# DeltaNet and SwiGLU on one core: the first inverse Z transposed as blocks side by side, spread by four masks, a quarter of it on GpSimd

## The chip, the cores and the metric

One core of a Trainium2 chip runs the kernel. The metric is the device time of one execution in microseconds (us). Three runs of the kernel before took 661.51, 661.8 and 662.65 us; their median is 661.8 us.

## The reference

Inputs: q, k, v of shape (4, 8, 768, 48) (batch, heads, positions, width), beta of (4, 8, 768), and three weights. All is float32.

```
k_n = k / (norm(k) + 1e-6)
for t in range(S):                       # S = 768, state (B, H, 48, 48) from zero
    y[t]  = q[t] @ state
    state = state + beta[t] * outer(k_n[t], v[t] - k_n[t] @ state)
x = y as (B*S, H*D) = (3072, 384)
out = (silu(x @ w_gate) * (x @ w_val)) @ w_out     # d_ff = 1536
```

## The kernel before, in words

The recurrence is computed in 12 chunks of 64 positions. Within a chunk, the sequential update is a triangular system: the matrix of products of the keys, scaled by beta over the squared norms, is inverted once, and then the chunk is matrix products. There are 32 pairs of batch and head, so a chunk has 32 matrices of 64x64. Two batches share the 128 partitions, 64 rows each. Once a chunk's output is there, the feed-forward part of its 256 tokens (gate, value, output) fills TensorE, while the next chunk's recurrence is woven in between.

The order of the instructions on each engine is written by hand (a manual schedule): each engine takes its instructions in the order of the program text, and waits at semaphores for the other engines. SyncE (SP) issues most of the transfers, in program order too.

The start is special, because nothing can fill TensorE until chunk 0 is through. The steps of it that matter here, in program order:

- `first_tiles` clears tiles and makes row masks from the identity (`m_rows`, and `m_low`, their negatives).
- `turned(c, ...)` transposes K or Q of a chunk on TensorE (L484) and ScalarE copies the result out of PSUM (L486, L488). `first_gram` multiplies K by itself; `first_diag` takes the 32x32 diagonal blocks into one tile, `flat`, by masks. `gram` and `gram_steps` do the products of later chunks and of Q with K (L498), with ScalarE copies (L518, L523).
- `low_copies(c, ...)` writes what lies below the 16x16 diagonal blocks of chunk c into `l_sb[c]`, negated by `m_low`: six ScalarE instructions (L667) for each of chunks 0 and 1, which share this first inversion.
- VectorE transposes `flat` in 32x32 blocks into `mb` (L1950). Afterwards a partition holds one matrix, and its elements lie along the free axis.
- `first_scale` multiplies by beta over the squared norms (L675, L680) and GpSimd writes the diagonal into `zb` (L676). `first_substitution` then inverts the 16x16 blocks by forward substitution: 15 steps of two VectorE instructions each (L700, L706).
- `first_z` transposes back (L710), and `spread_z` writes the blocks into `ztp[0]`, the operand Z of the products, with a mask that keeps the blocks on the diagonal (L723 on ScalarE, L725 on VectorE); chunk 0's part is spread here, chunk 1's inside `first_advance`.
- `unread(n, p)` issues n products (L633) whose result nobody reads. They keep TensorE occupied.
- `n_products` multiplies `l_sb` by Z (L733). It opens `first_advance`, the chain of products and copies by which chunk 0 becomes the input of the feed-forward part (L952, L1040); the first feed-forward products are L1562.

Beside this, `stage(n, after)` brings in weight pieces. For a piece with `after`, GpSimd copies one word (L261) of an earlier piece's place into the new place, so that the piece's transfer (L262, on SP) is issued only once the earlier piece has landed:

```
if after is not None:
    nc.gpsimd.tensor_copy(place[:, 0:1], staged[after][:, 0:1])
queue.dma_start(out=place, in_=...)
```

The loop that stages pieces 0 to 5 stands behind `first_scale` and ahead of `first_substitution`; `power_step` (L274, L280, ScalarE) and `convert` (L293, L301, L313, VectorE) later turn a landed piece into the weights used. GpSimd also masks the Q products of chunk 0 (`under_mask`, L537).

Of the kernel before, what the change touches and what calls it, by code (L numbers as in the profile page):

```python
# [8 lines left out]
FP32 = mybir.dt.float32  # L9
U32 = mybir.dt.uint32  # L10
ALU = mybir.AluOpType
ACTF = mybir.ActivationFunctionType

C = 64
DP = 64
R = 32
# [4 lines left out]
def kernel(  # L21
# [25 lines left out]
    nc = tc.nc  # L47
# [4 lines left out]
    NB = B // 2  # L52
# [5 lines left out]
    HH = NB * H  # L58
# [3 lines left out]
    const = ctx.enter_context(tc.tile_pool(name="const", bufs=1))  # L62
# [60 lines left out]
    ztp = [const.tile([128, 2, HH, C], FP32, name=f"zt{i}") for i in range(ZB)]  # L123
# [55 lines left out]
    def load_v(c):  # L179
        vin[c] = work.tile([128, 2, NB, NJ, D], FP32, name="vin", bufs=2)  # L180
        for b in range(2):
            src = halves(v, c, b).rearrange("bp (j par) p d -> par p (bp j) d", par=2)
            for par in range(2):
                s = half_of(b ^ par if c > 1 else b).start
                nc.sync.dma_start(  # L185
                    out=vin[c][s : s + 64, par].rearrange("p bp j d -> p (bp j) d"),
                    in_=src[par],
                )
# [28 lines left out]
    staged, powers, places = {}, {}, {}  # L217

    def words(tile_):
# [3 lines left out]
    places = {  # L223
        "z0": zt_flat[0],
        "z1": zt_flat[1],
        "wo": words(wo_sb).rearrange("p t d -> p (t d)"),
    }
    H_ = PIECE
# [12 lines left out]
    for n, (name, lo) in enumerate(place_of):  # L241
        m = 2 * pieces[n][4]
# [7 lines left out]
        at = max(before) if before else LATE.get(name, -1)  # L250
# [78 lines left out]
    for b in range(2):  # L329
        rows = mask_q[64 * b : 64 * b + 64]  # L330
        nc.gpsimd.affine_select(
            out=rows,
# [5 lines left out]
            channel_multiplier=-1,  # L338
        )

    m_rows = const.tile([128, 4], FP32, name="m_rows")
    m_low = const.tile([128, 3], FP32, name="m_low")
    m_two = const.tile([128, 4, 2], FP32, name="m_two")

    p_places = [const.tile([128, 1024], FP32, name=f"p_sb{i}") for i in range(2)]
    spent, late_loads = [], []
# [105 lines left out]
    def banks(name, tag):  # L452

        if type(tag) is int:
            return [ps_ffn([128, 512], name, tag + i) for i in range(2)]
        p = ps_pair(name, tag)
        return [p[:, 0], p[:, 1]]
# [86 lines left out]
    def gram(*args):  # L544
        for _ in gram_steps(*args):
            pass
# [11 lines left out]
    def new_mb():  # L558
        return work.tile([128, R, R], FP32, name="mb", bufs=1)
# [41 lines left out]
    def pairs_of_blocks(flat):  # L601

        v = flat.rearrange("p (b n) -> p b n", b=2)[:, :, 0 : B16 * R]
        return v.rearrange("p b (k i) -> p b k i", i=R)

    def first_tiles():
        a = work.tile([128, C * 2 * HH], FP32, name="a_sb")
        for c in range(2):
            l_sb[c] = a[:, R * R * c : R * R * (c + 1)].rearrange(
                "p (h k) -> p h k", k=C  # L610
            )
        first_of["flat"] = new_mb().rearrange("p k i -> p (k i)")
        first_of["zb"] = places["z1"].bitcast(FP32)[:, 4 * H_ - 1056 : 4 * H_]
        first_of["mb"] = places["wo"].bitcast(FP32)[:, 2 * H_ : 2 * H_ + 1056]
        nc.vector.memset(first_of["zb"], 0.0)
        for c in range(2):
            nc.vector.memset(l_sb[c][:, :, 48:C], 0.0)
        for x, rows in enumerate((slice(16, C), slice(R, C), slice(48, C), slice(0, R))):
            nc.vector.tensor_reduce(
                out=m_two[:, x],  # L620
                in_=ident.rearrange("p (b n) -> p b n", b=2)[:, :, rows],
                axis=mybir.AxisListType.X,
                op=ALU.add,
            )
        nc.vector.tensor_tensor(
            out=m_rows, in0=m_two[:, :, 0], in1=m_two[:, :, 1], op=ALU.add
        )
        nc.vector.tensor_scalar_mul(m_low, m_rows[:, 0:3], -1.0)

    def unread(count, p, m=512):  # L630

        for _ in range(count):
            nc.tensor.matmul(p[0:R, 0:m], half, half[:, 0:1].to_broadcast([128, m]))  # L633
# [11 lines left out]
    def first_diag(c, p, between=None):  # L645
        to = first_of["flat"].rearrange("p (j c par h) -> p c par j h", c=2, par=2, j=R)
        to = to[:, c]
        p = [p_h.rearrange("p x h j -> p x j h") for p_h in p]
        for par in range(2):
            nc.scalar.mul(to[:, par], p[par][:, 0], m_rows[:, 3:4])  # L650
            if between and par == 0:
                between()
        for par in range(2):
            nc.vector.scalar_tensor_tensor(
                out=to[:, par],
                in0=p[par][:, 1],
                scalar=m_rows[:, 1:2],
                in1=to[:, par],
                op0=ALU.mult,
                op1=ALU.add,  # L660
            )

    def low_copies(c, p):
        l_v = l_sb[c].rearrange("p (par h) k -> p par h k", par=2)
        for par in range(2):
            for x in range(3):
                nc.scalar.mul(  # L667
                    l_v[:, par, :, B16 * x : B16 * x + B16],
                    p[par][:, x // 2, :, B16 * (x % 2) : B16 * (x % 2) + B16],
                    m_low[:, x : x + 1],  # L670
                )

    def first_scale(r_b):
        zb, b = first_of["zb"], beta_b[:, 0]
        nc.vector.tensor_tensor(out=b, in0=b, in1=r_b, op=ALU.mult)  # L675
        nc.gpsimd.tensor_copy(zb[:, 0 : R * R : R + 1], b)  # L676
        mb = pairs_of_blocks(first_of["mb"])[:, :, :, 0:B16]
        for x in range(2):
            at = slice(B16 * x, B16 * x + B16)
            nc.vector.scalar_tensor_tensor(  # L680
                out=mb[:, x],
                in0=mb[:, x],
                scalar=-1.0,
                in1=b[:, None, at].to_broadcast([128, B16, B16]),
                op0=ALU.mult,
                op1=ALU.mult,
            )

    def first_substitution():

        zb, mb = pairs_of_blocks(first_of["zb"]), pairs_of_blocks(first_of["mb"])
        for j in range(B16 - 1):
            m = B16 - 1 - j
            shape = [128, 2, m, j + 1]
            t_v = tmp_of[nc.vector][:, 0 : 2 * (j + 1) * m].rearrange(
                "p (b i k) -> p b i k", b=2, i=m
            )
            z_v = zb[:, :, j + 1 : B16, 0 : j + 1]
            m_v = mb[:, :, j : j + 1, j + 1 : B16].rearrange("p b o i -> p b i o")
            nc.vector.tensor_tensor(  # L700
                out=t_v,
                in0=zb[:, :, j : j + 1, 0 : j + 1].to_broadcast(shape),
                in1=m_v.to_broadcast(shape),
                op=ALU.mult,
            )
            nc.vector.tensor_tensor(out=z_v, in0=z_v, in1=t_v, op=ALU.add)  # L706

    def first_z():
        z = new_mb().rearrange("p k i -> p (k i)")
        nc.vector.transpose(z, first_of["zb"][:, 0 : R * R])  # L710
        first_of["z"] = z.rearrange("p (i m) -> p i m", i=R)

    def spread_z(c, x, engine, bps=slice(0, NB)):

        def by_bp(t):
            t = t.rearrange("p (par bp j) i -> p par bp j i", par=2, bp=NB)[:, :, bps]
            return t.rearrange("p par bp j i -> p par (bp j) i")

        z_v = by_bp(first_of["z"].rearrange("p i (c h) -> p c h i", c=2)[:, c])
        out = by_bp(ztp[0][:, c, :, R * x : R * x + R])  # L720
        mask = m_rows[:, 1:2] if x else m_rows[:, 3:4]
        if engine is nc.scalar:
            nc.scalar.mul(out, z_v, mask)  # L723
        else:
            engine.tensor_scalar_mul(out, z_v, mask)  # L725

# [213 lines left out]
    def first_advance():  # L940
# [63 lines left out]
        for bp in range(NB):  # L1004
# [6 lines left out]
            )  # L1011
            plus(uu[:, :, bp], t[:, 1:3, bp], pairs[bp])
        spread_z(1, 0, nc.vector)
        held_loads[26] = lambda: load_v(2)
        yield
        pq = p_sb.pop(0)
# [25 lines left out]
            if bp == 0:  # L1042
                unread(1, banks("p_t", 0)[1], 256)
        unread(1, banks("p_t", 0)[1], 256)
        spread_z(1, 1, nc.scalar)
        yield
        p_s = of_state(0, uu)
        nc.scalar.copy(state, p_s)
# [870 lines left out]
    with tc.manual_schedule(  # L1919
# [26 lines left out]
        spread_beta(copy_a)  # L1946
        turned(0, True, 0)
        low_copies(0, p_g[0])
        low_copies(1, p_g[1])
        nc.vector.transpose(first_of["mb"][:, 0 : R * R], first_of["flat"])  # L1950
        r_b = first_n()
        first_scale(r_b)
# [4 lines left out]
        turned(2, False, "py")  # L1957
        first_q = [gram_steps(0, True, 0, (copy_a, copy_a))]
        next(first_q[0])
        gram(2, False, "px", (copy_a, copy_a))  # L1960
        turned(3, False, "py")
        turned(1, True, "px")
# [1 line left out]
        first_q.append(gram_steps(1, True, "px", (copy_a, copy_a)))  # L1964
        next(first_q[1])
        next(first_q[0])
        unread(4, banks("p_t", 2)[0])
        first_substitution()
        first_z()
        some, others = slice(0, 1), slice(1, NB)  # L1970
        spread_z(0, 1, nc.scalar, some)
        spread_z(0, 0, nc.vector, some)
        spread_z(0, 0, nc.vector, others)
        spread_z(0, 1, nc.vector, others)
        scale_v(0)
        next(first_q[1])
        next(first_q[0])
# [129 lines left out]
```

## Time and profile before

| | |
|---|---|
| median of 3 runs | 661.8 us (661.51 to 662.65) |
| profiled execution, its own time | 663.32 us |
| its span, first to last instruction | 661.6 us |
| mean granted TensorE clock | 0.995 |
| TensorE busy | 649.8 us |
| VectorE, ScalarE, GpSimd busy | 475.0, 281.3, 198.7 us |

The times of single instructions come from the one profiled execution. PE is TensorE, PEld its weight loads, DVE is VectorE, ACT ScalarE, POOL GpSimd, SP SyncE (SPq: its queue of transfers). A number such as L733 is a line of the kernel; in the changed kernel the same code stands a few lines earlier or later. In a timeline a row gives the start, the length, the engine, the line, what is written and read, and in brackets the idle time ahead of it and what ended it. The granted clock is 1.00 at full TensorE speed.

### The profile page before, as it was taken

To read this page: it belongs to the slowest core of one execution; us is meant where nothing else is said; L and a number is where in the kernel's file an instruction comes from. 1 tells how busy PE (TensorE), PEld (TensorE's weight loads), DVE (VectorE), ACT (ScalarE), POOL (GpSimd) and SP (SyncE) were. 2 spreads that over 40 slices of the span, in tenths; PEclk is the share of its full clock that TensorE was granted. 3 is DMA by queue.
4 is the path that set the end of the run, shared out by engine and by line. 5 is a ranking of instruction groups with operands and counts; after the bars stand their busy time and mean duration, and the time that the engine had idled before them with its cause. 6 is when DMAs were issued, how large, how long until landed. Compare 5 with 4: busy or idle time off the path is not lost.

```text
span 661.6 us, 24916 instructions
## 1 busy us (share of the span) xinstructions
PE 649.8 (98%) x10854; PEld 596.5 (90%) x10854; DVE 475.0 (72%) x989; ACT 281.3 (43%) x626; POOL 198.7 (30%) x312
## 2 busy tenths in 40 slices
PE   8989999999999999999999999999999999999997
PEld 4667888767999999999999999999999999999997
DVE  6779699999689767758667758667758655655563
ACT  4887757224435433434532533532433432333230
POOL 8030041013894032880031881030882000000000
PEclk8989999999999999999999999999999999999999
DMA  9659763005742451364464264364263442232220
GB/s 138 144 165 265 214 145 119 1 14 92 201 78 73 97 122 51 84 142 89 99 127 92 61 152 104 81 131 105 62 142 88 93 109 67 58 97 65 81 72 25
DMA packets 147438, 68.57 MB, mean 104 GB/s; under 512 B 123456, under 2 KB 126560, under 8 KB 147328
## 3 DMA queue, kind: packets, MB, share of 16 engines
q1 hardware_dynamic: 144832, 66.28, 42.8%
q8 instruction: 85, 1.39, 0.9%
q10 hardware_dynamic: 2240, 0.59, 0.5%
q0 software_dynamic: 256, 0.10, 0.2%
q14 instruction: 25, 0.20, 0.1%
HBM read 59.08 MB, written 7.86 MB: 101 GB/s over the span
## 4 chain that ended last, share of the span: by engine, by line
PE 86%; DVE 7%; SPq 3%; issue 2%; DMA 1%; ACT 1%; POOL 0%; DVEq 0%; ACTq 0%; POOLq 0%
PE ffn L1405 39%; PE ffn L1682 21%; PE ffn L1562 9%; PE ffn L1591 2%; SPq L139 2%; PE p_px L1167 2%; PE p_py L498 1%; DVE x_t L583 1%; DVE zb L589 1%; PE p_px L921 1%; PE p_py L1069 1%; PE p_py L1086 1%; PE p_px L1150 1%; PE p_px L498 1%; SPq L185 1%
## 5 line engine op out<-in xcount | busy, mean ns | idle before, releaser
L1405 PE MATMUL ffn<-x_t,w_gv 128*128 128x128 f32 x800 | 108.7, 279 | 0.9 <-DVE p_sb L1632 0.8
L1405 PEld LDWEIGHTS ffn<-x_t,w_gv 128*128 128x128 f32 x800 | 97.4, 192 | 4.1 <-DVE p_sb L1632 2.0
L1439 ACT ACTIVATE sil<-ffn 128x256 f32<-128x256 f32 x100 | 36.4, 383 | 115.3 <-PE ffn L1405 108.0
L1405 PE MATMUL ffn<-x_ffn,w_gv 128*128 128x128 f32 x640 | 84.6, 275 | 0.0
L1682 PE MATMUL ffn<-wo_sb,h_f 128*128 128x192 f32 x480 | 83.9, 328 | 0.0
L1682 PEld LDWEIGHTS ffn<-wo_sb,h_f 128*128 128x128 f32 x480 | 77.9, 190 | 0.6
L1405 PEld LDWEIGHTS ffn<-x_ffn,w_gv 128*128 128x128 f32 x640 | 78.0, 192 | 0.3
L820 POOL TENSOR_TENSOR n_b<-mb,half 128x32 f32<-128x32 f32 x5 | 27.9, 5582 | 161.4 <-DVE mb L552 161.4
L583 POOL TENSOR_TENSOR h_f<-zb,mb 128x31 f32<-128x31 f32 (+15 forms) x124 | 69.4, 559 | 19.2 <-PE p_py L798 6.0
L589 POOL TENSOR_TENSOR zb<-zb,h_f 128x31 f32<-128x31 f32 (+15 forms) x124 | 70.8, 571 | 9.7
L1405 PE MATMUL ffn<-x_t,h_f 128*128 128x128 f32 x472 | 64.7, 280 | 0.0
L1405 PEld LDWEIGHTS ffn<-x_t,h_f 128*128 128x128 f32 x472 | 57.3, 192 | 1.6 <-DVE ffn L1632 0.5
L1440 DVE TENSOR_TENSOR h_f<-sil,ffn 128x256 f32<-128x256 f32 x100 | 39.3, 418 | 24.0 <-ACT sil L1439 24.0
L1101 ACT COPY x_ffn<-p_py 32x256 f32<-32x256 f32 (+3 forms) x108 | 39.4, 365 | 29.0 <-PE p_py L1086 27.3
L1632 DVE TENSOR_TENSOR ffn<-p_sb,ffn 128x512 f32<-128x512 f32 x40 | 27.8, 696 | 25.9 <-PE ffn L1405 25.2
L1635 DVE TENSOR_TENSOR ffn<-ffn,p_sb 128x512 f32<-128x512 f32 x40 | 27.5, 691 | 19.9 <-PE ffn L1405 19.0
L1682 PE MATMUL ffn<-last_k,h_f 128*128 128x192 f32 x200 | 36.0, 327 | 0.0
L1635 DVE TENSOR_TENSOR o_sb<-o_sb,ffn 128x192 f32<-128x192 f32 x50 | 17.5, 350 | 24.2 <-PE ffn L1682 23.5
L1562 PE MATMUL ffn<-x_t,w_gv 128*128 128x256 f32 x144 | 33.9, 385 | 0.2 <-DVE x_t L1041 0.2
L1682 PEld LDWEIGHTS ffn<-last_k,h_f 128*128 128x128 f32 x200 | 32.9, 190 | 0.1
L1562 PE MATMUL ffn<-x_ffn,w_gv 128*128 128x256 f32 x144 | 31.9, 380 | 0.0
L1405 PE MATMUL ffn<-x_ffn,h_f 128*128 128x128 f32 x232 | 30.9, 276 | 0.0
(330 smaller groups left out, 1171.8 us busy)
## 6 DMA issues: line engine op xcount, KB each, us to landing
h_f<-w_s SPq DMA_DIRECT2D x81, 256.0 KB, 2.8
more_w<-w_s SPq DMA_DIRECT2D x27, 256.0 KB, 2.7
vin<-in_v_dram SPq DMA_DIRECT2D x48, 96.0 KB, 3.5
out_dram<-o_sb SPq DMA_DIRECT2D x46, 96.0 KB, 2.2
kn<-in_k_dram SPq DMA_DIRECT2D x20, 192.0 KB, 4.5
zt<-in_moe_w_out_dram SPq DMA_DIRECT2D x10, 384.0 KB, 4.2
qpad<-in_q_dram SPq DMA_DIRECT2D x36, 64.0 KB, 3.0
w_s<-h_f SPq DMA_DIRECT2D x7, 256.0 KB, 2.6
```

What stands on the lines that cost most here:

```text
L139: dmas[b % len(dmas)].dma_start(out=t[64 * b : 64 * b + 64, :, :, 0:D].rearrange("p bp h d -> p (bp h) d"), in_=halves(x, c, b).rearrange( ...
L583: engine.tensor_tensor(out=t_v, in0=zb[:, 0 : j + 1, j : j + 1].to_broadcast([128, j + 1, m]), in1=mb[:, j : j + 1, j + 1 : R].to_broadcas ...
L589: engine.tensor_tensor(out=zb[:, 0 : j + 1, j + 1 : R], in0=zb[:, 0 : j + 1, j + 1 : R], in1=t_v, op=ALU.add,)
L820: nc.gpsimd.tensor_tensor(out=n, in0=mb.rearrange("p j i -> p (j i)")[:, 0 : R * R : R + 1], in1=half, op=ALU.pow,)
L1101: nc.scalar.copy(x_all[at % 128 : at % 128 + rows, at // 128].rearrange("p (bp b i) -> p bp b i", bp=NB, b=2), p[64 * half + lo : 64 * hal ...
L1405: nc.tensor.matmul(p[:, u], w(u), moving, start=start and u == 0, stop=True, skip_group_check=True,)
L1439: nc.scalar.activation(silu_of, p[:, 0:2], ACTF.Silu)
L1440: nc.vector.tensor_tensor(out=h_of(c, PAIRS[r][e % 3], e // 3), in0=silu_of, in1=p[:, 2:4], op=ALU.mult)
L1562: nc.tensor.matmul(ps[name][:, i], w_sb[:, t, (f + i) * 128 : (f + i + 1) * 128], xts[c][:, t], start=(t == 0 and i == 0), stop=(t == KT - 1),
L1632: nc.vector.tensor_tensor(out=out, in0=a, in1=b, op=ALU.subtract)
L1635: nc.vector.tensor_tensor(out=out, in0=a, in1=b, op=ALU.add)
L1682: nc.tensor.matmul(p[x, part], a(f - f % 2)[:, f % 2], b(f), start=not begun and f == 0, stop=f == FH - 1, skip_group_check=True,)
```

## The change

- The 16x16 blocks of `zb` are laid out side by side (16 rows of 32 columns) instead of on the diagonal of 32x32; the transpose takes 512 columns instead of 1024, and the clearing 528 instead of 1056.
- The result is spread by four masks, one for each 16 rows of 64 (three new masks in `m_rows`), into 16 columns each, instead of two masks into 32 columns each. For chunk 0 ScalarE does one quarter, GpSimd one, VectorE two; for chunk 1 VectorE and ScalarE do two each.
- The negative sign of the scaled blocks moves into the masks of `first_diag`; `first_scale` scales only the columns that the substitution reads, rows 0 to 3 on VectorE and rows 4 to 14 on GpSimd, and the diagonal is copied by VectorE.
- `low_copies(1, ...)` is split into two parts of three ScalarE instructions and moved behind the Q product of chunk 0 and behind the copies of that product. The four `unread` products after it go to the bank pair `py` instead of bank 2.

```diff
@@ first_tiles
-        first_of["zb"] = places["z1"].bitcast(FP32)[:, 4 * H_ - 1056 : 4 * H_]
+        first_of["zb"] = places["z1"].bitcast(FP32)[:, 4 * H_ - 528 : 4 * H_]
...
-        for x, rows in enumerate((slice(16, C), slice(R, C), slice(48, C), slice(0, R))):
+        starts = (slice(16, C), slice(R, C), slice(48, C), slice(0, R))
+        quarters = [slice(B16 * x, B16 * x + B16) for x in range(3)]
+        for x, rows in enumerate(list(starts) + quarters):
...
-        nc.vector.tensor_scalar_mul(m_low, m_rows[:, 0:3], -1.0)
+        nc.vector.tensor_scalar_mul(m_low, m_rows[:, 0:4], -1.0)
@@ first_diag
-            nc.scalar.mul(to[:, par], p[par][:, 0], m_rows[:, 3:4])
+            nc.scalar.mul(to[:, par], p[par][:, 0], m_low[:, 3:4])
...
-                scalar=m_rows[:, 1:2],
+                scalar=m_low[:, 1:2],
...
-    def low_copies(c, p):
+    def low_copies(c, p, pars=range(2)):
@@ first_scale
-        nc.gpsimd.tensor_copy(zb[:, 0 : R * R : R + 1], b)
-        mb = pairs_of_blocks(first_of["mb"])[:, :, :, 0:B16]
-        for x in range(2):
-            at = slice(B16 * x, B16 * x + B16)
-            nc.vector.scalar_tensor_tensor(
-                out=mb[:, x],
-                in0=mb[:, x],
-                scalar=-1.0,
-                in1=b[:, None, at].to_broadcast([128, B16, B16]),
-                op0=ALU.mult,
-                op1=ALU.mult,
-            )
+        diag = zb[:, 0 : B16 * (R + 1)].rearrange("p (i n) -> p n i", i=B16)
+        b_v = b.rearrange("p (x i) -> p x i", x=2)
+        nc.vector.tensor_copy(diag[:, 0 : B16 + 1 : B16], b_v)
+        mb = pairs_of_blocks(first_of["mb"])
+        for engine, js in ((nc.vector, slice(0, 4)), (nc.gpsimd, slice(4, B16 - 1))):
+            m = mb[:, :, js, js.start + 1 : B16]
+            in1 = b_v[:, :, None, js.start + 1 : B16].to_broadcast(list(m.shape))
+            engine.tensor_tensor(out=m, in0=m, in1=in1, op=ALU.mult)
@@ first_substitution
-        zb, mb = pairs_of_blocks(first_of["zb"]), pairs_of_blocks(first_of["mb"])
+        zb = first_of["zb"][:, 0 : B16 * R].rearrange("p (i x k) -> p x i k", x=2, k=B16)
+        mb = pairs_of_blocks(first_of["mb"])
@@ first_z
-        z = new_mb().rearrange("p k i -> p (k i)")
-        nc.vector.transpose(z, first_of["zb"][:, 0 : R * R])
+        z = new_mb().rearrange("p k i -> p (k i)")[:, 0 : B16 * R]
+        nc.vector.transpose(z, first_of["zb"][:, 0 : B16 * R])
@@ spread_z
-        mask = m_rows[:, 1:2] if x else m_rows[:, 3:4]
+        z_v = first_of["z"][:, c]
+        out = ztp[0][:, c, :, B16 * y : B16 * y + B16]
+        mask = m_rows[:, 4 + y : 5 + y] if y < 3 else m_rows[:, 2:3]
...
+        elif engine is nc.gpsimd:
+            mask = mask[:, :, None].to_broadcast([128, HH, B16])
+            engine.tensor_tensor(out=out, in0=z_v, in1=mask, op=ALU.mult)
@@ first_advance
         spread_z(1, 0, nc.vector)
+        spread_z(1, 1, nc.vector)
...
-        spread_z(1, 1, nc.scalar)
+        spread_z(1, 2, nc.scalar)
+        spread_z(1, 3, nc.scalar)
@@ the order at the start
         low_copies(0, p_g[0])
-        low_copies(1, p_g[1])
...
         next(first_q[0])
+        low_copies(1, p_g[1], (0,))
         gram(2, False, "px", (copy_a, copy_a))
...
         next(first_q[0])
-        unread(4, banks("p_t", 2)[0])
+        low_copies(1, p_g[1], (1,))
+        unread(4, banks("p_t", "py")[0])
         first_substitution()
         first_z()
-        some, others = slice(0, 1), slice(1, NB)
-        spread_z(0, 1, nc.scalar, some)
-        spread_z(0, 0, nc.vector, some)
-        spread_z(0, 0, nc.vector, others)
-        spread_z(0, 1, nc.vector, others)
+        spread_z(0, 3, nc.scalar)
+        spread_z(0, 2, nc.gpsimd)
+        spread_z(0, 0, nc.vector)
+        spread_z(0, 1, nc.vector)
```

More of the change, by code (lines that the diff above doesn't have):

```diff
@@ L339 @@
         )
-    m_rows = const.tile([128, 4], FP32, name="m_rows")
-    m_low = const.tile([128, 3], FP32, name="m_low")
-    m_two = const.tile([128, 4, 2], FP32, name="m_two")
+    m_rows = const.tile([128, 7], FP32, name="m_rows")
+    m_low = const.tile([128, 4], FP32, name="m_low")
+    m_two = const.tile([128, 7, 2], FP32, name="m_two")
     p_places = [const.tile([128, 1024], FP32, name=f"p_sb{i}") for i in range(2)]
@@ L661, in first_diag @@
             )
-    def low_copies(c, p):
+    def low_copies(c, p, pars=range(2)):
         l_v = l_sb[c].rearrange("p (par h) k -> p par h k", par=2)
-        for par in range(2):
+        for par in pars:
             for x in range(3):
@@ L708, in first_z, with spread_z @@
     def first_z():
-        z = new_mb().rearrange("p k i -> p (k i)")
[L710 to L720, printed above, removed]
-        mask = m_rows[:, 1:2] if x else m_rows[:, 3:4]
+        z = new_mb().rearrange("p k i -> p (k i)")[:, 0 : B16 * R]
+        nc.vector.transpose(z, first_of["zb"][:, 0 : B16 * R])
+        first_of["z"] = z.rearrange("p (i c h) -> p c h i", i=B16, c=2)
+    def spread_z(c, y, engine):
+        z_v = first_of["z"][:, c]
+        out = ztp[0][:, c, :, B16 * y : B16 * y + B16]
+        mask = m_rows[:, 4 + y : 5 + y] if y < 3 else m_rows[:, 2:3]
         if engine is nc.scalar:
             nc.scalar.mul(out, z_v, mask)
+        elif engine is nc.gpsimd:
+            mask = mask[:, :, None].to_broadcast([128, HH, B16])
+            engine.tensor_tensor(out=out, in0=z_v, in1=mask, op=ALU.mult)
         else:
```

## The prediction

> **What bounds the kernel now.** I read the page first (share of each engine), then busy time by stretches of the span, then the timeline around the changed lines engine by engine, then the order and the semaphore waits of the changed program's instructions. On the page:
>
> ```profile
> PE 649.8 (98%) x10854; PEld 596.5 (90%) x10854; DVE 475.0 (72%) x989; ACT 281.3 (43%) x626; POOL 198.7 (30%) x312
> ```
>
> TensorE is busy nearly throughout, so what counts is when it starts its dense work and where it stands still. The stretches (us; busy time and instructions of PE, PEld, DVE, ACT, POOL; granted clock; DMA share; GB/s):
>
> ```profile
> 25.00:30.00 5.00, 5.00 (x111) 2.17 (x104) 3.15 (x5) 3.50 (x8) 0.67 (x3) 1.00 0.45 133
> 30.00:35.00 5.00, 3.73 (x198) 3.18 (x189) 3.77 (x8) 4.28 (x11) 2.90 (x4) 1.00 0.43 136
> 35.00:41.70 6.70, 5.69 (x130) 3.75 (x129) 4.24 (x11) 5.18 (x13) 0.91 (x6) 0.75 0.41 123
> 41.70:50.00 8.30, 7.63 (x209) 6.16 (x210) 6.62 (x18) 8.24 (x22) 2.22 (x6) 1.00 0.68 207
> 50.00:60.00 10.00, 10.00 (x282) 8.38 (x281) 9.86 (x33) 7.96 (x22) 0.34 (x1) 1.00 0.99 236
> ```
>
> All that the change touches lies before 48 us. From 41.7 us TensorE has only some 3 us of idle time until 600 us, none of it put down to a transfer, so a shift of the dense work is a shift of the end. Between 28.8 and 41.7 us runs the chain of chunk 0 (products, copies, products) that leads there. It starts with `n_products` (L733). What holds it? The timeline of TensorE alone:
>
> ```profile
> 24.15 1.16 PE L498 MATMUL p_px<-qt,kt 64*64 64x64 f32 x64
> 25.24 3.63 PE L633 MATMUL ffn<-half 128*32 128x512 f32 x8
> 28.80 1.16 PE L733 MATMUL ffn<-zt,a_sb 64*64 64x64 f32 x64
> 29.78 0.63 PE L952 MATMUL p_px<-vin,zt 64*64 64x48 f32 x32
> ```
>
> L733 follows the four filler products (L633, `unread`) without a gap. Its operand Z was ready earlier, as the timeline of VectorE and ScalarE shows:
>
> ```profile
> 24.90 1.25 DVE L710 STREAM_TRANSPOSE mb<-zt 128x1024 f32<-128x1024 f32 x1
> 26.18 0.75 ACT L723 ACTIVATE zt<-mb,m_rows 128x256 f32<-128x256 f32 x1
> 26.18 1.15 DVE L725 TENSOR_SCALAR zt<-mb,m_rows 128x256 f32<-128x256 f32 x3
> ```
>
> Z is done at 27.33 us, 1.47 us ahead of L733: a faster Z alone brings nothing. Now GpSimd, which gets a quarter of Z:
>
> ```profile
> 15.40 0.50 POOL L676 COPY zt<-beta_b 128x32 f32<-128x32 f32 x1 [1.00 <-DVE beta_b L675]
> 25.96 0.19 POOL L261 COPY h_f<-h_f 128x1 uint32<-128x1 uint32 x1 [10.06 <-DMA h_f<-in_moe_w_gate_dram]
> 27.95 0.29 POOL L261 COPY h_f<-h_f 128x1 uint32<-128x1 uint32 x1 [1.80 <-DMA h_f<-in_moe_w_val_dram]
> 28.89 0.18 POOL L261 COPY h_f<-h_f 128x1 uint32<-128x1 uint32 x1 [0.65 <-DMA h_f<-in_moe_w_gate_dram]
> 32.10 0.18 POOL L261 COPY h_f<-h_f 128x1 uint32<-128x1 uint32 x1 [3.02 <-DMA h_f<-in_moe_w_val_dram]
> 32.24 2.77 POOL L537 TENSOR_TENSOR p_sb<-p_sb,mask_q 128x512 f32<-128x512 f32 x2
> ```
>
> The four L261 copies are the one-word copies of `stage(2)` to `stage(5)`, each waiting until a weight piece has landed (pieces 0, 1, 2, 3). They stand ahead of `first_substitution` in the program. In the changed program's order the new spread on GpSimd is the instruction right behind the fourth of them, and the first `n_products` matmul has a wait on GpSimd that it did not have.
>
> **The change part by part.**
>
> Masks and clearing: three more reductions (L619, 0.53 us for four, so +0.4 us) and a half-size memset of `zb` (0.94 us for 1056 columns). VectorE then idles 1.94 us for K at 5.71 us: nothing.
>
> `first_scale`: out go two scalings on VectorE (0.77 us) and GpSimd's copy of the diagonal (0.50 us, to 15.90 us). In come, on VectorE, a copy of 32 columns (about 0.2, as L675 0.19) and a product of 120 columns (L700 of 128x120, 0.28), and on GpSimd a product of 242 columns beside them (L583 of up to 247 columns averages 0.80, so about 0.7). The substitution, which began at 16.24, begins near 15.9; GpSimd's rows are first read in its fifth step, which came 2.1 us after its first. Gain about 0.35 us, or a loss of 0.3 if VectorE and GpSimd hold each other up; either way it is spent in front of a wait with slack.
>
> Transpose: 512 columns for 1024, 1.25 to about 0.65 us. Spreads of chunk 0: VectorE two of 256 (0.44 each) for three, ScalarE one of 256 (0.75) as before. VectorE's part of Z is then ready near 26.0 instead of 27.33 us.
>
> Lower copies of chunk 1: six ScalarE copies of 0.25 us (17.21 to 18.9) move behind the copies of `turned(2)` (three of them) and behind `p_sb` of chunk 0 (the other three). The transposed K of chunk 2 comes out some 0.8 us earlier; down the alternation of TensorE and ScalarE (gram 2, chunk 3's transposes, gram 3, Q of chunk 1) I get the fillers' start at about 24.45 instead of 25.24, their end at about 28.05. The fillers change bank and now wait for the last copy out of `py` (25.16 before, about 24.35 after), which comes just ahead. ScalarE's spread, with the three copies before it, ends near 27.0. All of this would let L733 begin at 28.05, 0.75 us earlier. That is the most that this change could have gained by itself.
>
> GpSimd's spread of 256 columns: it cannot begin before the fourth L261 is through. That copy waits for piece 3, whose issue waits in turn for the second copy, so the landing stays at 32.05 whatever the arithmetic does:
>
> ```profile
> 22.96 0.43 SPq L262 DMA_DIRECT2D h_f<-in_moe_w_val_dram  x1
> 26.17 0.33 SPq L262 DMA_DIRECT2D h_f<-in_moe_w_gate_dram  x1
> 28.27 0.33 SPq L262 DMA_DIRECT2D h_f<-in_moe_w_val_dram  x1
> ```
>
> The spread takes the place of L537 at 32.24. Its cost: L583 of 128x256 0.65, L589 0.73, half of L537 0.70; I take 0.70, so Z is whole at 32.95 and L733 starts at about 33.05. Against 28.80 that is **+4.25 us**. The landing of a piece took 2.6 to 5.0 us from its issue in these rows, so I allow 0.75 either way. Behind the spread GpSimd's two L537 products and later L261 copies slip 0.7 us, and with them the issue of pieces 6 onward (35.23 to about 36); ScalarE first reads piece 6 at 42.4 us, which slips by more. What the chain needs next slips with TensorE: products, copies and conversions of pieces 0 to 5 stand in order behind `n_products` on VectorE and ScalarE.
>
> Chunk 1's spread: VectorE two of 0.44 for one of 0.66, before 1.01 us of idle time: nothing. ScalarE two of 0.75 for one of 1.18, +0.3 us where ScalarE is busy 8.24 of 8.30 us; I take +0.1.
>
> Clock: TensorE stands still from about 28.05 to 33.05. What less than that does is seen in three 1-us stretches (same columns):
>
> ```profile
> 36.00:37.00 1.00, 0.49 (x29) 0.39 (x24) 1.00 (x4) 0.49 (x2) 0.00 (x0) 0.94 0.71 186
> 37.00:38.00 1.00, 1.00 (x50) 1.00 (x44) 0.58 (x2) 0.28 (x1) 0.00 (x0) 0.50 0.87 309
> 40.00:41.00 1.00, 1.00 (x6) 0.37 (x5) 0.00 (x0) 1.00 (x2) 0.27 (x2) 0.85 0.44 78
> ```
>
> After a thin stretch (34 to 37 us) the granted clock is 0.50 from 36.9 to 40.3 us. A pair of L952 products then took 1.83 us (36.69 to 38.52) against 1.11 at full clock (29.78 to 30.89). I expect a new half-clock stretch of this length over `n_products` and the first pair: 0.75 (1.16 us scaled by 1.83/1.11) and 0.72, some 1.0 to 1.5 us on the chain. The old one may move or go; it costs about 0.9 us now (0.72 of the pair, and part of the slower transposes and fillers). Net between 0 and +1.5; I take +0.8, near the middle, since the rows show both lengths of the pair but not where the next thin stretch will fall. [...]
>
> Sum: 4.25 + 0.8 + 0.1, less about 0.2 for TensorE's "issue" gaps (0.28 and 0.54 us in the chain) that a standing engine may hide: **+5.0 us**. The profiled execution took 663.32 us with a span of 661.6, so 1.7 lies around the span; its span would become 666.6. The median of the runs, 661.8, is 1.5 below that execution, and I add the difference to the median: 666.8 us.
>
> **The rivals.**
>
> *The spread is not late (opposite side).* If piece 3 landed by 27.1 us, GpSimd would be done by 28.05, L733 would start 0.75 us earlier, and if the denser chain also lost the half-clock stretch, another 0.9: 661.1 or 660.2 us. For it: only one execution is seen. Against it: the landing would have to come 5 us earlier, before its own issue at 28.27. Chance 0.07, in equal parts 0.035 without and 0.035 with the clock's gain.
>
> *Absorbed in part.* The chain catches up because copies and conversions that stood in it are already through while TensorE waits, and the old half-clock stretch goes without a new one on the chain: +1.5 to +2.5, about 663.8. For it: conversions on VectorE sit in the chain at 31.45 and 34.60. Against it: they are queued behind `n_copies`, so they wait as well. Chance 0.06.
>
> *Worse.* Two more half-clock stretches, one over the dense products after 41.7 us (3.4 us at half clock loses 1.7): +7.5 or more, 669.5. Chance 0.06.
>
> **How the numbers follow.** The forecast, a late quarter of Z, has 0.81. Its own bounds are 4.25 with 0.75 either way, the clock from -0.9 to +1.5 and ScalarE's 0.3: 664.4 to 668.4. The range reaches a little to both neighbours: 664.0 to 669.2. A measurement of this kernel can tell about 0.2%, 1.3 us, from no change. Slower by more than that: forecast, worse and absorbed, 0.93 in all, of which I move 0.01 to "same" for the low end of absorption, so 0.92. Same: 0.035 and that 0.01, 0.045. Faster: 0.035.
>
> **What would show it.** Right: on GpSimd the spread right behind the fourth L261 at about 32.2 us; on TensorE idle time of 4 to 5 us before `n_products`, released by GpSimd, and fillers that end about 0.75 us earlier; `n_products` at half clock; the transpose at 0.65 us; the same dense stretch from about 46.7 instead of 41.7 us. Wrong: `n_products` starting below 30 us, a spread on GpSimd ahead of the staging copies, or a gap before `n_products` that is made up before the dense stretch.

## The result, and the profile after

The changed kernel takes 666.8 us (median of 6 runs, 665.56 to 667.72) against 662.22 us for the kernel before in the same comparison (6 runs, 661.36 to 664.01). The recorded ratio is 1.0051, 95% interval 1.0031 to 1.0070 (the quotient of these two medians is 1.0069): slower, by half a per cent. Medians, here and below, count every run, while ratios leave out two slow ones: 1080.0 us at a granted clock of 0.557, which was the profiled run of the quarter alone, and 670.39 us of the kernel before with cut transfers. The profiled execution of the changed kernel took 667.72 us with a span of 666.0, 4.4 us more than the 661.6 of before.

The timeline of GpSimd in the changed kernel (columns as in the prediction):

```profile
15.46 0.71 POOL L685 TENSOR_TENSOR wo_sb<-wo_sb,beta_b 128x242 f32<-128x242 f32 x1 [1.01 <-DVE beta_b L677]
26.48 1.18 POOL L261 COPY h_f<-h_f 128x1 uint32<-128x1 uint32 x2 [10.32 <-DMA h_f<-in_moe_w_gate_dram]
30.30 0.18 POOL L261 COPY h_f<-h_f 128x1 uint32<-128x1 uint32 x1 [2.65 <-DMA h_f<-in_moe_w_gate_dram]
30.97 0.18 POOL L261 COPY h_f<-h_f 128x1 uint32<-128x1 uint32 x1 [0.48 <-DMA h_f<-in_moe_w_val_dram]
31.11 0.75 POOL L721 TENSOR_TENSOR zt<-mb,m_rows 128x256 f32<-128x256 f32 x1
```

The spread L721 stands right behind the fourth staging copy. TensorE in the same stretch, with its waits below (time waited in total, times, longest):

```profile
23.01 3.63 PE L635 MATMUL p_py<-half 128*32 128x512 f32 x8
31.91 1.98 PE L731 MATMUL ffn<-zt,a_sb 64*64 64x64 f32 x64 [5.26 <-POOL zt L721]
...
PE ffn L731 <- POOL zt L721: 5.3, 1, 5.3
PE p_px L950 <- issue: 1.6, 2, 1.1
```

The fillers (L635) end at 26.64 us, then TensorE stands still for 5.26 us until GpSimd is done. VectorE and ScalarE had delivered their three quarters by 26.6 us:

```profile
25.08 0.71 DVE L709 STREAM_TRANSPOSE mb<-zt 128x512 f32<-128x512 f32 x1
25.83 0.79 DVE L723 TENSOR_SCALAR zt<-mb,m_rows 128x256 f32<-128x256 f32 x2
```

The five stretches of the prediction, now of the changed kernel (us; busy time of PE, PEld, DVE, ACT, POOL; granted clock; DMA share; GB/s):

```profile
25.00:30.00 5.00, 1.65 (x4) 0.22 (x2) 2.42 (x5) 2.35 (x5) 1.18 (x2) 0.87 0.52 173
30.00:35.00 5.00, 3.09 (x116) 3.09 (x120) 0.92 (x2) 0.80 (x2) 3.78 (x7) 0.50 0.40 134
35.00:41.70 6.70, 4.32 (x220) 3.81 (x213) 4.35 (x11) 5.14 (x13) 0.67 (x4) 0.96 0.60 183
41.70:50.00 8.30, 7.97 (x108) 4.84 (x112) 5.73 (x15) 7.03 (x20) 1.80 (x6) 0.59 0.70 211
50.00:60.00 10.00, 9.88 (x328) 8.49 (x320) 7.88 (x24) 8.56 (x20) 0.00 (x0) 1.00 0.78 197
```

TensorE's 5.00 us of work between 25 and 30 have become 1.65. The clock then stands at 0.50 through 30 to 35 us, and again over most of 41.7 to 50, where the first dense products now fall. They begin at 47.05 us instead of 41.75, and the first six take 2.59 us instead of 1.73 (the kernel before, then the changed one):

```profile
41.75 1.73 PE L1562 MATMUL ffn<-x_t,w_gv 128*128 128x256 f32 x6 [0.19 <-DVE x_t L1041]
47.05 2.59 PE L1562 MATMUL ffn<-x_t,w_gv 128*128 128x256 f32 x6
```

### The profile page after: what moved, and what is told of

Same layout as the page of the kernel before. It is cut to its first block, busy times and chain, and to the rows that moved or that the text cites. A ratio compares the mean times of both kernels' runs of the same rounds, so it can differ in the third digit from the quotient of the medians.

```text
span 666.0 us, 24921 instructions
## 1 busy us (share of the span) xinstructions
PE 650.0 (98%) x10854; PEld 597.7 (90%) x10854; DVE 474.2 (71%) x992; ACT 281.4 (42%) x627; POOL 199.1 (30%) x313
## 4 chain that ended last, share of the span: by engine, by line
PE 86%; DVE 7%; SPq 3%; issue 1%; DMA 1%; ACT 1%; POOL 0%; DVEq 0%; ACTq 0%; POOLq 0%
PE ffn L1405 39%; PE ffn L1682 21%; PE ffn L1562 9%; PE ffn L1591 2%; SPq L139 2%; PE p_px L1167 2%; PE p_py L498 1%; DVE x_t L583 1%; DVE zb L589 1%; PE p_py L1069 1%; PE p_px L919 1%; PE p_py L1086 1%; PE p_px L1150 1%; PE p_px L498 1%; SPq L185 1%
## 5 line engine op out<-in xcount | busy, mean ns | idle before, releaser
L1405 PEld LDWEIGHTS ffn<-x_t,w_gv 128*128 128x128 f32 x800 | 97.4, 192 | 3.9 <-DVE p_sb L1632 1.8
L1562 PE MATMUL ffn<-x_ffn,w_gv 128*128 128x256 f32 x144 | 31.9, 380 | 0.0
L1562 PEld LDWEIGHTS ffn<-x_t,w_gv 128*128 128x128 f32 x144 | 27.3, 195 | 4.7 <-ACT w_gv L274 0.8
```

The lines of the kernel that those rows point to most:

```text
L1405: nc.tensor.matmul(p[:, u], w(u), moving, start=start and u == 0, stop=True, skip_group_check=True,)
L1562: nc.tensor.matmul(ps[name][:, i], w_sb[:, t, (f + i) * 128 : (f + i + 1) * 128], xts[c][:, t], start=(t == 0 and i == 0), stop=(t == KT - 1),
```

## The experiments

Theory 1: the quarter on GpSimd is late because it is queued behind the four staging copies, each waiting for a transfer, and that wait makes the loss. Rivals: the other parts of the change make it; the clock makes it; GpSimd is slow in itself. The ratios below are to the kernel before, measured in the same comparison; its median there was 663.05 us for the quarter taken from GpSimd, the quarter alone, the staging behind the spread and the nine fillers, 662.27 for the longer queue, the changed kernel once more and the two other parts, and 663.24 for the cut transfers. Among runs of one kernel the times spread over several us, so the traces carry the verdicts as much as the times.

**The quarter taken from GpSimd** (changed kernel, three of four spreads on VectorE):

```diff
-        spread_z(0, 2, nc.gpsimd)
         spread_z(0, 0, nc.vector)
+        spread_z(0, 2, nc.vector)
```

> The changed kernel with GpSimd's quarter of chunk 0's spread given to VectorE (three of four there). Theory 1, the quarter is late because it is queued behind the four staging copies: with it gone, L731 starts at about 27.0 us (fillers end at 26.64, VectorE's third quarter at about 26.9) instead of 31.91, the half-clock stretch before it goes, and the time is 660 to 661.5 us, at or under the kernel before. Rival, the side-by-side layout, the masks or the moved lower copies cost the time themselves: it stays above 664.5 us.

Measured: 662.53 us, ratio 0.9989 (0.9965 to 1.0013). The loss is gone, but the 660 to 661.5 us that were expected were not reached. TensorE's timeline:

```profile
27.29 1.22 PE L731 MATMUL ffn<-zt,a_sb 64*64 64x64 f32 x61 [0.43 <-DVE zt L723]
...
30.87 0.51 PE L950 MATMUL p_px<-v,qpad 64*64 64x48 f32 x21 [0.87 <-issue]
34.87 0.88 PE L950 MATMUL p_px<-x_t,qpad 64*64 64x48 f32 x22 [1.09 <-issue]
```

L731 starts at 27.29 us, 1.5 us earlier than in the kernel before, yet the interval of the ratio does not show it faster than that kernel. Part of the 1.5 us is given back a little later, where TensorE waits for nothing that the profile shows ("issue"): 0.87 and 1.09 us where the kernel before had 0.28 and 0.54:

```profile
31.69 0.51 PE L952 MATMUL p_px<-v,qpad 64*64 64x48 f32 x21 [0.28 <-issue]
35.15 0.51 PE L952 MATMUL p_px<-x_t,qpad 64*64 64x48 f32 x21 [0.54 <-issue]
```

**The quarter alone** (kernel before, one of VectorE's spreads given to GpSimd):

```diff
-        spread_z(0, 0, nc.vector, others)
+        spread_z(0, 0, nc.gpsimd, others)
```

with a GpSimd branch in `spread_z` (here two instructions of 128 columns).

> The kernel before with one of its three VectorE spreads of chunk 0 given to GpSimd (two instructions of 128 columns), nothing else of the change. Theory 1: the wait alone makes the loss; GpSimd's spread stands behind the fourth staging copy at about 31 to 32 us, L733 starts at about 32 to 33 us instead of 28.8, and the time is 665.5 to 668 us. Rival, the loss comes from other parts: 662 to 663 us.

Measured: 668.49 us, ratio 1.0068 (1.0046 to 1.0091). A later execution of it was profiled:

> The same kernel as only_quarter, for an undisturbed profile of it. Theory 1: GpSimd's spread right behind the fourth staging copy, at 30.5 to 32.5 us, and L742 (the first products with Z) right behind it, 2.5 to 4.5 us later than in the kernel before, with TensorE idle until then. Rival, the products start by 29 us and the loss lies elsewhere.

Its span was 667.2 us. On GpSimd, and as TensorE's longest wait:

```profile
31.89 0.18 POOL L261 COPY h_f<-h_f 128x1 uint32<-128x1 uint32 x1 [1.86 <-DMA h_f<-in_moe_w_val_dram]
32.03 0.89 POOL L727 TENSOR_TENSOR zt<-mb,m_rows 128x128 f32<-128x128 f32 x2
...
PE ffn L742 <- POOL zt L727: 4.0, 1, 4.0
```

The first 32 records of L742, which need the other half of Z, ran at 27.83 us; the rest stood for 4.0 us. So the quarter behind the staging copies is enough for the loss, and by the experiment before the rest of the change makes none that can be measured. That the length of the wait sets the size of the loss is not shown by this; the longer queue below speaks against it.

**The staging behind the spread** (changed kernel; pieces 2 to 5 are staged after `spread_z`, pieces 0 and 1 where they were):

```diff
-        for n in range(6):
-            stage(n, n - 2 if n > 1 else None)
+        for n in range(2):
+            stage(n)
...
         spread_z(0, 1, nc.vector)
+        for n in range(2, 6):
+            stage(n, n - 2)
```

> The changed kernel with the staging of pieces 2 to 5 (GpSimd copy and transfer) moved behind the spread in program order; GpSimd keeps its quarter. Theory 1: GpSimd's spread starts with VectorE's, at about 25.9 us, L731 at about 26.7, pieces 2 to 5 are issued at most 0.7 us later than in the changed kernel, and the time is 660 to 661.5 us. [...] Second rival, late pieces cost what the spread gains: conversions wait and the time is 663 or more.

Measured: 664.66 us, ratio 1.0020 (0.9993 to 1.0047), runs from 662.29 to 668.0. The start came out as expected, the time did not: six of the twelve runs lie between 662.29 and 663.84 us, six between 665.49 and 668.0, and the profiled one (665.49) is of the second six. Its first spread on VectorE, GpSimd's spread, and TensorE's longest waits:

```profile
25.88 1.09 DVE L723 TENSOR_SCALAR zt<-mb,m_rows 128x256 f32<-128x256 f32 x1
25.92 0.81 POOL L721 TENSOR_TENSOR zt<-mb,m_rows 128x256 f32<-128x256 f32 x1 [9.71 <-DVE mb L709]
...
PE p_px L950 <- issue: 2.9, 2, 2.2
PE p_px L1194 <- issue: 2.1, 1, 2.1
```

GpSimd's spread runs beside VectorE's in 0.81 us, so GpSimd is not slow in itself, and L731 follows the fillers at 27.62. VectorE pays for it, though: its spread beside GpSimd's took 1.09 us, where one alone takes 0.43 (L723 in the changed kernel). Its two spreads took 1.44 us here, and all three took 1.14 us when VectorE had them alone (the first experiment), so even in time the quarter on GpSimd saves VectorE nothing. The fillers, which end later, hide this. But "issue" gaps of 2.9 and 2.1 us follow, where the kernel before had 0.8 and 0.7, and the clock stood at 0.50 from 34.4 to 44.7 us. The second rival of the expectation, late pieces, is not what TensorE waits for by the profile, and pieces 2 to 5 were not issued later (27.05 to 31.13 us, in the changed kernel 27.56 to 31.18).

**A longer queue** (changed kernel; piece 6, a fifth copy, also staged ahead of the spread):

```diff
-        for n in range(6):
+        for n in range(7):
```

> The changed kernel with a fifth staging copy (piece 6, which waits for piece 4) ahead of GpSimd's spread instead of behind it. Theory 1, the queue in front of the spread sets the start: piece 4 lands at 33 to 34 us, so the spread moves from 31.1 to about 33.7 us, L731 to about 34.5, and the time goes up by about 2.6 us on the changed kernel, to 669 to 671 us where the changed kernel takes 667. Rival, the wait does not set the time any more (other gaps take up the difference): within 1 us of the changed kernel.

The start came as expected: the spread at 33.60 us, L731 at 34.41, waiting 8.0 us for GpSimd. The time did not follow: 667.52 us, ratio 1.0080 (1.0057 to 1.0103), beside 667.02 us and 1.0076 (1.0056 to 1.0095) for the changed kernel in the same comparison:

> The changed kernel once more, beside the other parts of this call. Theory 1: L731 waits for GpSimd by 4 to 6 us; the time is 3.5 to 5 us over the kernel before, ratio 1.005 to 1.0075. Rival: the first comparison was a draw of the clock and the ratio is below 1.003.

So the rival holds here: `n_products` starts 2.6 us later than in the repeated changed kernel (34.41 against 31.82), and that costs nothing that can be measured. By the spread of the six runs of each, an extra cost of up to about 2 us would not show (my estimate). In the two traces the dense products start 2.28 us later (47.75 against 45.47), but one "issue" gap, at L1194, is 0.77 us instead of 3.22, and the spans are 667.4 and 667.7 us.

**No idle time in the wait** (changed kernel, nine fillers instead of four):

```diff
-        unread(4, banks("p_t", "py")[0])
+        unread(9, banks("p_t", "py")[0])
```

> The changed kernel with nine filler products instead of four (0.91 us each at full clock, so they end at about 31.2 us, still before GpSimd's quarter at 31.86). The wait is unchanged, TensorE is not idle in it. Theory 1 with a clock term: L731 still starts near 32 us but at full clock (1.16 us, not 1.98), the half-clock stretch at 28 to 35 us is gone, and the time is 1.0 to 2.5 us under the changed kernel, 664.3 to 665.8 us. Rival, the clock costs nothing (the wait explains all): 666.5 us or more.

Measured: 668.77 us, ratio 1.0080 (1.0053 to 1.0107): no gain. L731 started at 32.03 us at full clock (1.16 us, not 1.98), the dense products at 43.91 instead of 47.05 us; then

```profile
59.87 1.52 PE L1194 MATMUL p_px<-v,zb 64*64 64x48 f32 x43 [2.85 <-issue]
...
56.00:60.00 4.00, 1.15 (x28) 0.69 (x30) 3.90 (x14) 1.24 (x4) 0.00 (x0) 0.91 1.18 200
60.00:64.00 4.00, 4.00 (x49) 3.40 (x50) 1.76 (x5) 0.80 (x1) 0.00 (x0) 0.50 0.85 319
```

2.85 us of "issue" and half a clock over the dense products behind it (59.3 to 66.1 us) took the 3.1 us back: the span is 667.4 us. By its number the rival holds; by the trace the clock did cost time, and it cost it at another place.

**The other parts alone.** The lower copies moved and split, in the kernel before:

> The kernel before with chunk 1's lower copies split and moved and the fillers in the other bank, nothing else. Theory 1: the fillers start about 0.75 us earlier, but Z is done at about 27.3 us as before, so L733 starts at about 28.0 to 28.1 (where the fillers end late) or 27.4 us, and the time is 0 to 0.8 us under the kernel before. Rival, the moved copies are part of the loss: 663.5 us or more beside 662.5 for the kernel before.

```diff
-        low_copies(1, p_g[1])
...
+        low_copies(1, p_g[1], (0,))
...
-        unread(4, banks("p_t", 2)[0])
+        low_copies(1, p_g[1], (1,))
+        unread(4, banks("p_t", "py")[0])
```

Measured: 663.46 us, ratio 1.0017 (0.9998 to 1.0036), inconclusive. L733 started at 26.93 us, after a wait of 0.31 us for ScalarE's spread. The layout, the masks and `first_scale` alone (the first experiment's kernel with the lower copies and the bank put back):

> The changed kernel with chunk 1's lower copies and the fillers' bank as in the kernel before, and GpSimd's quarter on VectorE: the side-by-side layout, the masks and first_scale alone. Theory 1: Z is done at about 27.2 us, the fillers end at 28.8 as in the kernel before, so L731 starts there and the time is the kernel before's, within 0.5 us. Rival, GpSimd's part of first_scale blocks VectorE for more than it saves and shows in the time: 663.5 us or more beside 662.5.

Measured: 662.32 us, ratio 0.9997 (0.9979 to 1.0015). The fillers, and with them L731, came at 27.99 us and not at 28.8; in this execution the half-clock stretch that the kernel before showed from 13 to 16.4 us was missing. Neither part costs what the whole change costs (4.6 us of medians): the upper ends of the two intervals stand for 2.4 and 1.0 us.

**Are the "issue" gaps late instruction blocks?** The gaps fall at fixed places in the instruction stream: in the kernel before, the first comes after 8 records of the second set of products of chunk 0's chain, the next after 8 of the fourth, 128 products and 128 weight loads later, 256 instructions. With five more fillers (10 products, 10 weight loads) the gap at L1194 left 43 records of its group to do instead of 33: it moved by as much as instructions were added. The page of the profile counts the transfers of instructions, the same 85 in every run here (queue, packets, MB, share of the DMA engines):

```profile
q8 instruction: 85, 1.39, 0.9%
```

TensorE's 10854 products and 10854 weight loads make 84.8 blocks of those 256, so these 85 transfers, of 16384 bytes each, fit TensorE's instructions. Their times in the traces settle the question. Twelve executions have 38 "issue" gaps of 0.19 us or more between 25 and 90 us, and every one of them ends 1.2 to 1.8 us after one of these transfers has landed (they land 3.4 to 10.5 us apart): in the kernel before 30.39 us for the gap that ends at 31.69 and 33.82 for 35.15, in the repeated changed kernel 60.51 for the 3.22 us that end at 62.17. By these times the gaps are waits for late blocks. Where two neighbouring blocks both come late in the chain of chunk 0 (seven executions), the second transfer starts 1.1 to 2.0 us after the first gap has ended, and from the end of one gap to the end of the next it takes 3.5 to 4.3 us. The 128 small products in between went no faster, so a chain that starts earlier gives part of its lead back here.

Whether weight transfers delay the blocks was tried by transferring only 32 of the 128 partitions of every piece from the 25th on:

```diff
+        rows = 32 if n >= 24 else 128
-            out=place, in_=src[t * 128 : (t + 1) * 128, f0 : f0 + m].bitcast(U32)
+            out=place[0:rows],
+            in_=src[t * 128 : t * 128 + rows, f0 : f0 + m].bitcast(U32),
```

> The kernel before with every weight piece from the 25th on transferred for 32 of its 128 partitions only (so part of the weights is wrong; the instructions and waits are the same). Theory 2, TensorE's gaps that no wait explains fall at the ends of blocks of 256 instructions and are late instruction blocks behind weight transfers: the gap at L1194 (0.74 us in the kernel before) falls under 0.3 us and the time by 0.5 to 1 us. Rival, the gaps have nothing to do with the transfers: they stay as they are, within what they vary.

> The changed kernel with the same cut of the transfers (part of the weights is wrong). Theory 1: the wait for GpSimd at 26 to 31.9 us is unchanged, since pieces 0 to 5 are whole, and the time stays 3.5 us or more above before_quarter_loads. Theory 2: the gap at L1194 (0 and 3.22 us in two executions of the changed kernel) is under 0.5 us. Rival: the gap at L1194 comes and goes as before.

Measured: 661.66 us, ratio 0.9987 (0.9963 to 1.0011), and 666.33 us, 1.0059 (1.0035 to 1.0083). The gap at L1194 was 1.86 us in the first, at a place where the kernel before had none (its 0.74 lies one block further), and 0.22 in the second. The test decides nothing about the weight transfers: the blocks that end these gaps had landed at 56.25 and 58.45 us, and the first of the cut transfers was issued only at 58.51 and 59.10. What makes the blocks late stays open. The difference between the two kernels stays at 4.67 us of medians, and the changed one still waits for GpSimd (4.49 us).

## Why the prediction was right

The forecast of 666.8 us rested on one reading: program order on GpSimd puts the spread behind four waits for transfers. That held in every kernel that kept the order. Where the engine changed, the loss went; where the order changed, the wait went, and the loss in half of the runs. That the forecast met the median to a tenth is luck, because its terms were off in both directions. From the kernel before to the changed one, in the profiled pair:

- To the start of `n_products`: +4.25 us set, +3.11 measured (31.91 against 28.80).
- From there to the dense products: +0.6 set (0.8 for the clock less 0.2 for the gaps), +2.19 measured (15.14 against 12.95).
- From there to the end: +0.1 set, -0.90 measured. In all 4.95 set and 4.4 measured.

The other execution of the changed kernel has +3.02, +0.70 and +2.38 in these places, 6.1 in all. By the steps of the prediction:

- The wait: the fourth staging copy started at 30.97 us instead of 32.10, so piece 3 landed 1.1 us earlier, which is more than the 0.75 us allowed. The spread itself took 0.75 us for the 0.70 of the sum. What stands behind it did not slip: piece 6 was issued at 34.48 us, not at about 36.
- The fillers' end: predicted 28.05, measured 26.64. The half-clock stretch at 13 to 16.4 us, which I had taken as part of the kernel, was absent; without it and with the copies in their old place (the layout alone) the fillers ended at 27.99. Of the 2.2 us to the 28.8 of before, about 0.8 is thus the clock, and the moved copies are worth up to 1.35 in these single executions, where 0.75 was set.
- The clock: `n_products` took 1.98 us for 1.16, +0.82 where 0.75 was set. The stretch at half clock was twice as long as taken (28.7 to 35.5 us), and a second one of the same length fell on the start of the dense products (42.3 to 49.2). The prediction had this only in its rival "worse". Here it did not add up to that rival, because of the next point. The rows of before show a stretch after thin work, but not that standing still for 5 us must bring one; it did come in all five executions with a wait of 4 us or more (`n_products` took 1.98 us in three of them and 1.49 in the changed kernel with cut transfers, and with the quarter alone the clock stood at 0.50 from 32 to 36 us).
- The "issue" gaps: taken as 0.2 us of gain, they are the term that was mis-sized. From `n_products` to 70 us the kernel before loses 2.37 us in them (0.28, 0.54, 0.62, 0.74, 0.19), the changed kernel 1.62 in one execution and 4.27 in another. In the profiled pair 1.55 us of gaps that the kernel before has behind 41.75 us are missing in the changed one, and stand against the half clock on its dense products.
- `first_scale`: the substitution began at 16.34 us, not 15.9. The prediction's loss case came true, with 0.1 us instead of 0.3, and as said it cost nothing.
- A shift of the dense work is a shift of the end: true of this pair to within 0.90 us, but not a rule. The longer queue moved the dense products by another 0.7 to 2.3 us (47.75 against 47.05 and 45.47 in two executions of the changed kernel) and the time by nothing that can be measured; the nine fillers brought them 3.1 us forward, and the time did not fall.
- The range: its two ends are not added up alike. 664.4 leaves out the 0.2 us of the gaps and lets the clock go to -0.9, where the working had it between 0 and +1.5; 668.4 has the 0.2 taken off.

Of the rivals, "not late" did not occur: in all seven traced executions whose spread stands behind the fourth copy, which waits for piece 3, that copy started between 30.0 and 31.9 us. Whether the rest of the change could gain 0.75 us is open: with the quarter on VectorE, L731 is 1.5 us earlier, and the interval of the ratio, 0.9965 to 1.0013, holds no gain as well as one of 0.75 us.

## What to carry to other kernels

Before giving a small operation to an engine that looks idle, read what stands ahead of it in that engine's program: here GpSimd was idle for ten microseconds, but idle in a wait for a transfer, and everything behind that wait is as late as the transfer. A head start or a delay of 2 to 3 us ahead of a dense stretch need not reach the end one for one, so the term of a sum that passes through such a stretch deserves a wide bound. Before splitting an operation between VectorE and GpSimd, measure both side by side: twice here the split saved VectorE no time (0.84 us against 0.77 in `first_scale`, and 1.44 us for two spreads against 1.14 for three). Where executions differ by several us, compare the step that was changed in the traces, and let the times only confirm it.

## What the runs showed of the hardware

VectorE was held up beside GpSimd in `first_scale`. The timeline of VectorE, whose second row runs beside L685 on GpSimd (15.46 to 16.17 us, shown above):

```profile
15.41 0.20 DVE L680 COPY zt<-beta_b 128x32 f32<-128x32 f32 x1
15.50 0.80 DVE L685 TENSOR_TENSOR wo_sb<-wo_sb,beta_b 128x120 f32<-128x120 f32 x1
19.14 0.28 DVE L699 TENSOR_TENSOR x_t<-zt,wo_sb 128x120 f32<-128x120 f32 x1
```

The product of 120 columns took 0.80 us; one of the same size later, with GpSimd idle, 0.28. VectorE's product ended 0.13 us after GpSimd's (16.30 against 16.17), a remainder shorter than the 0.28 us that it takes alone. The split scaling took 0.84 us (15.46 to 16.30), where the two scalings of the kernel before took VectorE 0.77 (15.37 to 16.14): it saved no time. The spread shows the same: VectorE's took 1.09 us beside GpSimd's, and 0.43 alone.

The half clock came in stretches of one, two or three times 3.4 us (36.9 to 40.3 us in the kernel before, 28.7 to 35.5 in the changed kernel, 34.4 to 44.7 with the staging behind the spread), at places that differ between executions. In the changed kernel the clock dropped about 2.1 us after TensorE had stopped at 26.64 (0.85 in the us from 28, 0.50 in the next); in the longer queue `n_products`, 8.0 us after the stop at 26.43, ran at half clock (1.98 us for 1.16). Whether the place of the stretches makes part of the spread of the times is not shown: no run here separates it from the "issue" gaps.

By their number and times the 85 transfers of 16384 bytes brought TensorE's instructions, and in stretches of small products (128 of them to a block) a late block cost between 0.19 and 3.22 us, ahead of products that waited for nothing else.
